# A decode-attention kernel: two loads merged, and matmuls added in TensorE's gaps at the end

## The chip, the cores and the metric

The kernel runs on one core of one Trainium2 chip. The metric is the device time of one execution in microseconds (us), taken over several executions; the span of a profile is about 2 us shorter, because it counts from the first to the last instruction. All runs quoted count as fast runs: the slower state that some programs show plays no part. Below, a "slow run" only means one that took about 1 us or more longer than the fastest of the same kernel. The variants of a group and the kernel before were timed alternately on one chip; the two groups of experiments ran on two different chips, so variants of different groups are compared by way of the kernel before, whose medians there differ by 0.01 us.

## The reference

One decoded token goes through two branches whose outputs are mixed by a scalar gate. Cut to what matters:

```python
q = (x @ wq)                       # 1 x 1024 times 1024 x 4096: 32 heads of 128
scores = q . k_cache / sqrt(128)   # 4 kv heads x 65536 keys x 128
o = softmax(scores) . v_cache      # 4 kv heads x 65536 values x 128
a = o @ wo                         # 4096 x 1024
z = gelu(x @ w_in)                 # 1024 x 3584
z1, z2 = halves of z;  z2 = layernorm(z2)
b = (z1 * (w_sp * z2 + b_sp)) @ w_out
out = g * a + (1 - g) * b          # g = sigmoid(sum(x * gate_w))
```

All inputs are bfloat16. The K and V caches are 134 MB of the 162 MB that have to be read, and every byte is used once: this is a job for the DMA engines.

## The kernel before

All large loads go through one helper. It issues a DMA from SyncE into a slice of one big SBUF buffer of five slots of 4 MB; `at` is the slot. A load can be issued when the readers of the slot's old contents are done.

```python
WO_SPLIT = ((16,), (8, 4, 2, 1, 1))

def load(src, shape, at):
    ...
    v = kv[:, int(at * CT * P):int(at * CT * P) + n]
    ...
    ins = nc.sync.dma_start(out=v, in_=src)
    ...

win_t = [load(win_view[:, i * KH:(i + 1) * KH, :], (KH, F), 3 + i) for i in range(2)]
wq_t = [load(wq_view[:, i * KH:(i + 1) * KH, :], (KH, HD), 1 - i) for i in range(2)]
```

The end of the kernel, which the argument is about: the last V tiles, the last head's normalisation (`head_out`: VectorE steps with two small matmuls between them), and then the output projection, in pieces of `wo` that shrink towards the end so that little work follows the last byte. A "row" of `wo` is here one 1024-column row on each of the 128 partitions, 256 KB. Each row costs four matmuls of 32 output partitions x 256 columns, which run side by side in the four column groups of the array: in the profile before, the four of the last row start within 0.01 us of one another, and each takes 0.37 to 0.40 us.

```python
def project(w, n, vec, c0, first=False, last=False):
    for c in range(n):
        for t in range(NB):                                    # NB = 4
            nc.tensor.matmul(
                out_ps[t * B:(t + 1) * B, :],
                lhsT=vec[:, c0 + c:c0 + c + 1].to_broadcast([P, B]),
                rhs=w[:, c, t * NO:(t + 1) * NO],
                start=(first and c == 0), stop=(last and c == n - 1), ...)

for j, n, at in ((0, 2, 1), (2, 1, 3), (3, 1, 4)):             # the last head's V: 2 + 1 + 1 tiles
    for i, vt in enumerate(load_kv(A_v_cache, G - 1, j, at, n)):
        v_tile(G - 1, j + i, vt)
head_out(G - 1)                                                # makes oa, the vector for wo
...
for at, split in enumerate(WO_SPLIT):
    for n in split:
        t = load(wo_view[:, c0:c0 + n, :], (n, D), at + c0 % (OC // 2) * D / (CT * P))
        project(t, n, oa, c0, last=(c0 + n == OC))
        c0 += n
```

## Time and profile before

| | kernel before |
|---|---|
| median of the first 6 runs | 383.28 us (383.12 to 383.5) |
| span of the profiled run | 381.4 us |
| load queue | 162.01 MB, 98.7% of the 16 DMA engines' span |
| TensorE busy, mean granted clock | 61%, 0.82 |

These are lines of the profile page of the kernel before. In the first two, one character is a fortieth of the span, in tenths; the third gives the load queue's packets, MB and share of the DMA engines' time; the last is the chain of waits by engine.

```profile
...
PEclk9966659998759895989588959895799679969766
DMA  9999999999999999999999999999999999999995
...
q1 hardware_dynamic: 4324, 162.01, 98.7%
...
DMA 59%; PE 20%; DVE 16%; issue 2%; ACT 1%; SPq 1%; DVEq 0%; ACTq 0%
...
```

The DMA engines are busy from start to end, so time can only go where the stream of bytes is not yet or no longer flowing, or where it is slowed. TensorE's granted clock (1.0 is 9 here, 0.5 is 5) rises and falls the whole time.

First, the last steps of the chain of waits (start, duration, what), then the `wo` matmuls on the timeline (start, duration, engine, line, operation, count, and in brackets the idle time before and what ended it), then the windows view: for each stretch its length, the busy time of the engines, the granted clock (PEclk), the DMA share and GB/s.

```profile
...
347.00 31.88 DMA kv<-in_A_wo_dram
...
378.92 0.43 PE out_ps L478 x3
...
379.37 0.37 ACT out_sb L521
...
```

```profile
...
370.37 4.62 PE L478 MATMUL out_ps<-kv,oa 128*32 128x256 bf16 x96 [1.39 <-DVE oa L469]
376.33 0.62 PE L478 MATMUL out_ps<-kv,oa 128*32 128x256 bf16 x16 [1.34 <-DMA kv<-in_A_wo_dram]
377.60 1.08 PE L478 MATMUL out_ps<-kv,oa 128*32 128x256 bf16 x12 [0.64 <-DMA kv<-in_A_wo_dram]
378.92 0.41 PE L478 MATMUL out_ps<-kv,oa 128*32 128x256 bf16 x4 [0.24 <-DMA kv<-in_A_wo_dram]
```

```profile
...
core 0: us, PE busy (x) PEld busy (x) DVE busy (x) ACT busy (x) POOL busy (x), PEclk, DMA share, GB/s
...
371.20:373.60 2.40, 2.40 (x53) 1.85 (x45) 0.00 (x0) 0.00 (x0) 0.00 (x0) 0.50 0.99 413
373.60:376.90 3.30, 1.96 (x56) 1.45 (x49) 0.00 (x0) 0.00 (x0) 0.00 (x0) 0.93 0.94 368
376.90:379.10 2.20, 1.25 (x20) 0.50 (x15) 0.00 (x0) 0.00 (x0) 0.00 (x0) 0.63 0.33 122
...
```

The chain says that from 347.00 to 378.88 the kernel waits for `wo` to arrive. When the last row is there, 0.43 us of matmul and 0.37 us of cast follow, then the output DMA. The timeline says that 96 matmuls, for the first 24 rows, are done by 375, because 16 of the rows were there early (in the DMA packet records their last packet ends at 368.38) and their 64 matmuls could run from 370.37 on. After that TensorE waits for each piece, if only for 0.07 us before the row that starts at 378.28: it is never behind. The windows view says that it does much of that at a granted clock of 0.50.

### The profile page before, as it was taken

How to read it: one execution, taken by the hardware profiler on the slowest of the kernel's cores; microseconds unless marked ns; L12 is line 12 of the kernel's file. 1: busy time of each engine (PE TensorE's matmuls, PEld its weight loads, DVE VectorE, ACT ScalarE, POOL GpSimd, SP SyncE). 2: the span in 40 equal slices, each digit the busy share in tenths (PEclk: the TensorE clock that was granted, in tenths of full speed). 3: DMA queues.
4: the chain of work that ended last, by engine and by line, in shares of the span. 5: the costliest groups of instructions: out<-in, count | busy, mean ns of one | idle time of the engine just before them, and what ended most of it. 6: DMA issues, size and time to landing. Idle time of an engine off the chain costs nothing.

```text
span 381.4 us, 2581 instructions
## 1 busy us (share of the span) xinstructions
PE 232.4 (61%) x1372; PEld 56.8 (15%) x796; DVE 218.4 (57%) x211; ACT 39.6 (10%) x55; POOL 4.4 (1%) x10
## 2 busy tenths in 40 slices
PE   0433467678157944796397629872967196849355
PEld 0110011112011210121011101120111011212123
DVE  4241487996687506966977059669780488550040
ACT  1010001111601100114010001050001010500000
POOL 4000000000000000000000000000000000000000
PEclk9966659998759895989588959895799679969766
DMA  9999999999999999999999999999999999999995
GB/s 376 439 426 416 433 436 440 436 461 429 400 426 440 440 435 426 440 440 440 440 428 440 440 440 433 428 427 406 433 440 428 426 433 427 440 411 436 440 405 230
DMA packets 4375, 162.17 MB, mean 425 GB/s; under 512 B 520, under 2 KB 524, under 8 KB 908
## 3 DMA queue, kind: packets, MB, share of 16 engines
q1 hardware_dynamic: 4324, 162.01, 98.7%
q8 instruction: 8, 0.13, 0.1%
q14 instruction: 3, 0.02, 0.0%
q10 hardware_dynamic: 40, 0.01, 0.0%
HBM read 162.01 MB, written 0.00 MB: 425 GB/s over the span
## 4 chain that ended last, share of the span: by engine, by line
DMA 59%; PE 20%; DVE 16%; issue 2%; ACT 1%; SPq 1%; DVEq 0%; ACTq 0%
DMA kv<-in_A_k_cache_dram 37%; PE s_ps L391 15%; DVE kv L384 9%; DMA kv<-in_A_wo_dram 8%; DMA kv<-in_A_wq_dram 7%; DMA kv<-in_A_v_cache_dram 7%; PE o_ps L437 3%; DVE pt L427 2%; DVE mx L386 1%; DVE o_sb L451 1%; PE q_ps L277 1%; ACT sc L424 1%; DVE rowt L447 1%; ACT sc L402 1%; SPq L167 1%
## 5 line engine op out<-in xcount | busy, mean ns | idle before, releaser
L391 PE MATMUL s_ps<-kv,wt 128*128 128x512 bf16 x512 | 142.1, 437 | 81.8 <-DVE kv L384 81.7
L384 DVE STREAM_TRANSPOSE kv<-kv 128x2048 int32<-128x2048 int32 x64 | 142.7, 2280 | 55.5 <-DMA kv<-in_A_k_cache_dram 55.5
L437 PE MATMUL o_ps<-kv,pt 128*64 128x512 bf16 x512 | 61.6, 399 | 7.7 <-DMA kv<-in_A_v_cache_dram 7.7
L391 PEld LDWEIGHTS <-wt 128*128 128x128 bf16 x256 | 27.5, 108 | 197.6 <-issue 140.2
L402 ACT CAST sc<-s_ps 128x1024 bf16<-128x1024 f32 x16 | 16.2, 1013 | 253.5 <-PE s_ps L391 253.5
L437 PEld LDWEIGHTS <-pt 128*64 128x64 bf16 x256 | 16.0, 115 | 50.7 <-issue 48.1
L427 DVE STREAM_TRANSPOSE pt<-sc 128x1024 bf16<-128x1024 bf16 x16 | 18.6, 1217 | 6.8 <-ACT sc L424 6.8
L386 DVE TENSOR_REDUCE mx<-sc 128x1 f32<-128x1024 bf16 x12 | 14.5, 1207 | 10.1 <-ACT sc L402 10.1
L424 ACT ACTIVATE sc<-sc,nb 128x1024 bf16<-128x1024 bf16 x16 | 18.2, 1137 | 12.2 <-DVE nb L420 12.2
L447 DVE TENSOR_TENSOR rowt<-o_ps,own 128x1024 f32<-128x1024 f32 x4 | 4.8, 1194 | 24.9 <-PE o_ps L437 24.9
L457 PE MATMUL om_ps<-o_sb,hsel 128*32 128x128 f32 x8 | 2.5, 421 | 19.7 <-DVE o_sb L451 19.7
L406 DVE TENSOR_REDUCE mx<-sc 128x1 f32<-128x1024 bf16 x4 | 4.9, 1220 | 14.2 <-ACT sc L402 14.2
L277 PE MATMUL q_ps<-kv,xT 128*32 128x512 bf16 x64 | 7.2, 627 | 7.4 <-DMA kv<-in_A_wq_dram 7.4
L478 PE MATMUL out_ps<-kv,oa 128*32 128x256 bf16 x128 | 6.7, 366 | 3.7 <-DMA kv<-in_A_wo_dram 2.2
L277 PE MATMUL z_ps<-kv,xT 128*32 128x448 bf16 x64 | 6.2, 570 | 3.8 <-DMA kv<-in_B_w_in_dram 3.8
L344 DVE TENSOR_TENSOR rowt<-q_ps,own_b 128x512 f32<-128x512 f32 x2 | 1.3, 686 | 12.5 <-PE q_ps L277 12.5
L451 DVE TENSOR_REDUCE o_sb<-rowt 128x128 f32<-128x1024 f32 x4 | 7.5, 1872 | 0.1
L292 DVE TENSOR_TENSOR rowt<-z_ps,own_b 128x448 f32<-128x448 f32 x2 | 1.2, 620 | 8.5 <-PE z_ps L277 8.5
L233 PE MATMUL xb_ps<-xg,spread 8*128 8x256 bf16 x1 | 0.4, 367 | 9.1 <-DMA xg<-in_gate_w_dram 9.1
L277 PEld LDWEIGHTS <-xT 128*32 128x32 bf16 x64 | 3.0, 139 | 19.4 <-issue 19.3
L478 PEld LDWEIGHTS <-oa 128*32 128x32 bf16 x128 | 4.4, 124 | 6.1 <-issue 3.3
L521 ACT CAST out_sb<-out_ps 128x256 bf16<-128x256 f32 x1 | 0.4, 372 | 45.4 <-PE out_ps L478 45.4
(88 smaller groups left out, 54.8 us busy)
## 6 DMA issues: line engine op xcount, KB each, us to landing
kv<-in_A_k_cache_dram SPq DMA_DIRECT2D x4, 4096.0 KB, 26.8
kv<-in_A_wq_dram SPq DMA_DIRECT2D x2, 4096.0 KB, 32.8
kv<-in_A_v_cache_dram SPq DMA_DIRECT2D x2, 4096.0 KB
kv<-in_B_w_in_dram SPq DMA_DIRECT2D x2, 3584.0 KB, 15.0
kv<-in_A_wo_dram SPq DMA_DIRECT2D x1, 4096.0 KB
kv<-in_B_w_out_dram SPq DMA_DIRECT2D x1, 3584.0 KB
kv<-in_A_wo_dram SPq DMA_DIRECT2D x1, 2048.0 KB, 28.6
kv<-in_A_wo_dram SPq DMA_DIRECT2D x1, 1024.0 KB, 30.7
```

What stands on the lines that cost most here:

```text
L277: ins = nc.tensor.matmul(ps[t * B:(t + 1) * B, k * HN:k * HN + n], lhsT=xT[:, i * KH + c:i * KH + c + 1].to_broadcast([P, B]), rhs=w[:, c, ...
L384: nc.vector.transpose(out=kb[:, v * n:(v + 1) * n], in_=kb[:, v * n:(v + 1) * n])
L386: nc.vector.reduce_max(**late.pop())
L391: ins = nc.tensor.matmul(s_ps[:, k * HN:(k + 1) * HN], lhsT=wt[g % 2][:, v, b].rearrange("p a v h -> p (a v h)"), rhs=kx[:, b // 2, b % 2, ...
L402: nc.scalar.copy(out=sct[g, j][:], in_=s_ps[:])
L406: nc.vector.reduce_max(**late.pop())
L424: nc.scalar.activation(out=sct[g, j][:], in_=sct[g, j][:], func=ACT.Exp, scale=SCALE, bias=nb[:, 0:1], accum_out=lss[g][:, j:j + 1])
L427: nc.vector.transpose(out=ptt[g, j][:].rearrange("p c x -> p (c x)"), in_=sct[g, j][:])
L437: ins = nc.tensor.matmul(o_ps[g][hs, e, :], lhsT=ptt[g, j][:, 2 * u:2 * u + 2, :].rearrange("p c x -> p (c x)"), rhs=vx[:, 2 * u + e], sta ...
L447: nc.vector.tensor_tensor(out=om8, in0=o_ps[g][:].rearrange("p e (v d) -> p (e v) d", d=DH), in1=own_8[:].unsqueeze(2).to_broadcast([P, 2 ...
L451: nc.vector.tensor_reduce(out=o_sb[:], in_=om8.rearrange("p x d -> p d x"), axis=AX.X, op=ALU.add)
L478: nc.tensor.matmul(out_ps[t * B:(t + 1) * B, :], lhsT=vec[:, c0 + c:c0 + c + 1].to_broadcast([P, B]), rhs=w[:, c, t * NO:(t + 1) * NO], st ...
```

## The change

The intent: fewer and larger loads (`w_in` in one, the first 24 rows of `wo` in one), and since TensorE then has gaps, matmuls that are thrown away ("fillers" below) keep it active so that its clock stays full for the 96 matmuls that now follow a single landing. The fillers multiply a weight buffer of which 15 of 16 elements are zero; nobody reads the result. There are 4 after the last V tile, 8 after the last head, and 2, 1 and 1 between the last rows.

```diff
--- before.py
+++ after.py
@@ -22,7 +22,8 @@
 CC = CT // VC
 ZN = 448
 HN = 512
-WO_SPLIT = ((16,), (8, 4, 2, 1, 1))
+WO_SPLIT = (24, 4, 2, 1, 1)
+WO_BUSY = (0, 2, 1, 1, 0)
 
 
 @with_exitstack
@@ -62,7 +63,7 @@
     SCALE = float(DH) ** -0.5
     assert NB * VC * REP == P and G * B == P and B == REP * QD and DH == P and D % P == 0
     assert S % (P * CT) == 0 and F == 2 * NB * ZN and ZN == B * FC and HD == NHB * NB * HN
-    assert NHB * NB == 2 * G and CC * B == 2 * HN and sum(map(sum, WO_SPLIT)) == OC
+    assert NHB * NB == 2 * G and CC * B == 2 * HN and sum(WO_SPLIT) == OC
 
     const = ctx.enter_context(tc.tile_pool(name="const", bufs=1))
     wk = ctx.enter_context(tc.tile_pool(name="wk", bufs=2))
@@ -186,7 +187,8 @@
 
     KH = KC // 2
     win_view = B_w_in.rearrange("(p c) n -> p c n", c=KC)
-    win_t = [load(win_view[:, i * KH:(i + 1) * KH, :], (KH, F), 3 + i) for i in range(2)]
+    win = load(win_view, (KC, F), 3)
+    win_t = [win[:, i * KH:(i + 1) * KH, :] for i in range(2)]
     wq_view = A_wq.rearrange("(p c) n -> p c n", c=KC)
     wq_t = [load(wq_view[:, i * KH:(i + 1) * KH, :], (KH, HD), 1 - i) for i in range(2)]
 
@@ -469,6 +471,15 @@
         nc.vector.tensor_scalar(out=oa[gs, :], in0=osum[gs, :], scalar1=rl[gs, 1:2],
                                 scalar2=gate[gs, :], op0=ALU.mult, op1=ALU.mult)
 
+    def keep_busy(n):
+        ps = pss.tile([P, 2 * HN], FP32, name="busy_ps", tag="s")
+        w = wt[G % 2][:].rearrange("p v b t u h -> p (v b t u h)")
+        for i in range(n):
+            ins = nc.tensor.matmul(ps[:, :HN], lhsT=w[:, :P], rhs=w[:, :HN], start=True,
+                                   stop=True, skip_group_check=True)
+            if i > 0:
+                same_weights(ins)
+
     NO = D // NB
     out_ps = psl.tile([P, NO], FP32, name="out_ps")
 
@@ -506,16 +517,18 @@
     for j, n, at in ((0, 2, 1), (2, 1, 3), (3, 1, 4)):
         for i, vt in enumerate(load_kv(A_v_cache, G - 1, j, at, n)):
             v_tile(G - 1, j + i, vt)
+    keep_busy(4)
     head_out(G - 1)
+    keep_busy(8)
 
 
     wo_view = A_wo.rearrange("(p c) n -> p c n", c=OC)
     c0 = 0
-    for at, split in enumerate(WO_SPLIT):
-        for n in split:
-            t = load(wo_view[:, c0:c0 + n, :], (n, D), at + c0 % (OC // 2) * D / (CT * P))
-            project(t, n, oa, c0, last=(c0 + n == OC))
-            c0 += n
+    for n, busy in zip(WO_SPLIT, WO_BUSY):
+        t = load(wo_view[:, c0:c0 + n, :], (n, D), c0 * D / (CT * P))
+        project(t, n, oa, c0, last=(c0 + n == OC))
+        keep_busy(busy)
+        c0 += n
     out_sb = const.tile([P, NO], BF16, name="out_sb")
     out_rows = out.rearrange("o t (q n) -> (o t q) n", n=NO)
     nc.scalar.copy(out=out_sb[:], in_=out_ps[:])
```

## The prediction

> **What bounds the kernel now.** The DMA stream. The page shows the DMA engines at 9 tenths or more in 39 of 40 slices, the load queue 98.7% busy, 162.0 MB at 425 GB/s over 381.4 us; its chain of waits is 59% DMA. The Trainium skill ("DMA: Bandwidth & Descriptors", "Where 436 GB/s comes from") gives a ceiling of 435 GB/s; the trace agrees (steady slices 426 to 440). Estimate from it: 162.0 MB / 435 GB/s = 372.4 us, so only about 9 us could go at all: 1 us before the first packet, slow first packets, short pauses of single DMA engines, 2 us of unequal finish of the engines, 2.5 us after the last row of wo (timeline: last matmuls 378.92, cast 379.37, output DMA 379.77, end 381.4). PE is 61% busy; at the tail the windows view shows a granted clock of 0.50 to 0.74.
>
> **Removed.** Two loads of 30. In the DMA packet records a 64 KB packet takes 2421 ns, a 32 KB one 1216, so a packet boundary costs about 11 ns; each merge removes eight packets per engine: 16 x 11 = 0.18 us, plus two completion packets of 9 ns. Estimate: 0.2 us off the DMA stream, all critical.
>
> **Moved, off the path.** The first w_in half's matmuls (3.2 us from 12.66) must now wait for all of w_in (about 19.7). The z chain ends 2 to 3 us later, but q's second half lands only at 39.1, and the K load freed by q's first half (issued 33.0) has 16 us of queue ahead of it. The 24-row wo load must wait for the V tile in the next buffer: issued at 345.2 instead of 333.1, with the queue filled until 358.7. No starvation in either.
>
> **Added.** 16 matmuls of 512 columns (0.22 us each at full clock, 0.43 at half). The Trainium skill ("TensorE: Matmul & The Clock Gate", Part 1) describes a free-running window of 3413 ns; the trace agrees (granted stretches are multiples of 3.41 us), and adds: from half clock, windows over 83% busy led to full, under 75% to half; from full clock, under 42% to half. Rows 16 to 23 of wo land at 373.8. Before, 64 of the first 96 matmuls were done by then; now all 96 start there: 24 groups x 0.107 = 2.6 us at full clock, 5.1 at half. The later rows land at 376.3, 377.6, 378.9. At full clock PE catches up, and the last group is 0.1 to 0.2 us shorter. But the 8 fillers end by 370.7 (full) or 372.4 (half), leaving 1.4 to 3 us idle before 373.8, so in some window phases the clock falls just when the 96 start; then fillers between the last rows delay the end by 0.3 to 1.5 us.
>
> **Sum.** -0.2 (DMA), -0.15 (tail at full clock), +0.3 or so averaged over phases, with more spread than before. I expect 383.0 us, 8 in 10 between 382.2 and 384.0: within 2% almost surely.
>
> **What would show it.** Right: load queue still about 98.7% busy; two loads and 256 packets fewer, last landing 0.1 to 0.4 us earlier; first q matmuls 1 to 3 us later but K landings unchanged. The granted clock in 374 to 379 decides: if full, the last project matmuls follow the last landing by under 0.5 us; if half, PE runs without a gap from 373.8 to the end, and the chain names project, not the wo DMA.
>
> **What would make it wrong.** Larger packets changing the DMA rate or the engines' unequal finish by over 1 us; instruction fetches shifting; a K load issued so late that the queue runs empty.

## The result

| | median us | lowest to highest | runs |
|---|---|---|---|
| before | 383.28 | 383.12 to 383.5 | 6 |
| changed | 384.59 | 383.04 to 385.24 | 6 |

The ratio is 1.0028 (95% interval 1.001 to 1.0046). Ratios here are the mean time of one kernel's fast runs over that of the other's of the same rounds, so they are not quite the ratios of the medians quoted. The change made the kernel slower by 0.3% in the ratio, clear of the noise; the median, 384.59, lies above the predicted range of 382.2 to 384.0. The six runs were 383.04, 385.24, 384.61, 384.66, 384.57 and 384.15: one slightly faster than any run before, five slower by 0.9 to 2.0 us.

The profiled run was the fast one, 383.04 us. Its page:

```profile
...
PEclk9997569998659885989598958996889588979789
...
q1 hardware_dynamic: 4036, 162.01, 98.7%
...
```

The load queue is as busy as before, with 288 packets fewer (256 of data and 32 that signal the completion of a load on one engine). The chain of waits, the timeline (the lines with `busy_ps` are fillers) and the windows of this fast run:

```profile
...
346.59 30.78 DMA kv<-in_A_wo_dram
...
378.73 0.32 PE out_ps L489 x4
...
```

```profile
...
369.21 1.90 PE L478 MATMUL busy_ps<-wt 128*128 128x512 bf16 x8
373.64 3.24 PE L489 MATMUL out_ps<-kv,oa 128*32 128x256 bf16 x112 [2.53 <-DMA kv<-in_A_wo_dram]
...
377.41 0.40 PE L489 MATMUL out_ps<-kv,oa 128*32 128x256 bf16 x8 [0.21 <-DMA kv<-in_A_wo_dram]
...
378.73 0.29 PE L489 MATMUL out_ps<-kv,oa 128*32 128x256 bf16 x4
```

```profile
...
371.20:373.60 2.40, 0.00 (x0) 0.00 (x0) 0.00 (x0) 0.00 (x0) 0.00 (x0) 1.00 0.81 338
373.60:376.90 3.30, 3.26 (x113) 3.05 (x112) 0.00 (x0) 0.00 (x0) 0.00 (x0) 1.00 0.92 363
...
```

This is what the change was meant to do. The granted clock is 1.00; the 112 matmuls of the first 28 rows take 3.24 us. The chain waits for `wo` until 377.37 and then follows matmuls and fillers that keep pace with the landings: the last matmuls start at 378.73. In the DMA packet records the last packet of the last row ends at 378.22 us instead of 378.37. So this run explains a gain of 0.2 us, and not the loss. The loss had to be caught in a profile of a slow run.

At the start, the later work on `w_in` is harmless. The timeline of the first 50 us, before and then changed (line 233/235 is the first small matmul, 277/279 the first half of q, 384/386 the first K tile):

```profile
...
9.13 0.37 PE L233 MATMUL xb_ps<-xg,spread 8*128 8x256 bf16 x1 [9.13 <-DMA xg<-in_gate_w_dram]
...
29.39 3.55 PE L277 MATMUL q_ps<-kv,xT 128*32 128x512 bf16 x32 [1.26 <-DMA kv<-in_A_wq_dram]
...
48.83 2.31 DVE L384 STREAM_TRANSPOSE kv<-kv 128x2048 int32<-128x2048 int32 x1 [1.59 <-DMA kv<-in_A_k_cache_dram]
```

```profile
...
13.14 0.36 PE L235 MATMUL xb_ps<-xg,spread 8*128 8x256 bf16 x1 [13.14 <-DMA xg<-in_gate_w_dram]
...
30.23 3.38 PE L279 MATMUL q_ps<-kv,xT 128*32 128x512 bf16 x32
...
48.69 2.31 DVE L386 STREAM_TRANSPOSE kv<-kv 128x2048 int32<-128x2048 int32 x1 [1.53 <-DMA kv<-in_A_k_cache_dram]
```

The first half of q starts 0.84 us later, the first K tile 0.14 us earlier.

### The profile page after: what moved, and what is told of

The parts are those of the page before. It is cut to its first block, busy times and chain, and to the rows that moved or that the text cites. A ratio compares the mean times of both kernels' runs of the same rounds, so it can differ in the third digit from the quotient of the medians.

```text
span 381.1 us, 2597 instructions
## 1 busy us (share of the span) xinstructions
PE 230.6 (60%) x1386; PEld 55.8 (15%) x801; DVE 218.4 (57%) x211; ACT 39.6 (10%) x55; POOL 4.4 (1%) x10
## 3 DMA queue, kind: packets, MB, share of 16 engines
q1 hardware_dynamic: 4036, 162.01, 98.7%
## 4 chain that ended last, share of the span: by engine, by line
DMA 57%; PE 22%; DVE 17%; issue 2%; ACT 1%; ACTq 0%; SPq 0%; DVEq 0%
DMA kv<-in_A_k_cache_dram 37%; PE s_ps L393 15%; DVE kv L386 9%; DMA kv<-in_A_wo_dram 8%; DMA kv<-in_A_v_cache_dram 7%; DMA wb<-in_B_b_sp_dram 5%; PE o_ps L439 3%; DVE pt L429 2%; PE z_ps L279 1%; DVE mx L388 1%; DVE o_sb L453 1%; PE q_ps L279 1%; ACT sc L426 1%; DVE rowt L449 1%; ACT sc L404 1%
## 5 line engine op out<-in xcount | busy, mean ns | idle before, releaser
L393 PE MATMUL s_ps<-kv,wt 128*128 128x512 bf16 x512 | 139.7, 432 | 84.4 <-DVE kv L386 84.3
L439 PE MATMUL o_ps<-kv,pt 128*64 128x512 bf16 x512 | 62.9, 405 | 6.8 <-DMA kv<-in_A_v_cache_dram 6.8
L489 PE MATMUL out_ps<-kv,oa 128*32 128x256 bf16 x128 | 4.2, 273 | 2.8 <-DMA kv<-in_A_wo_dram 2.7
L279 PE MATMUL z_ps<-kv,xT 128*32 128x448 bf16 x64 | 4.9, 484 | 0.0
L489 PEld LDWEIGHTS <-oa 128*32 128x32 bf16 x128 | 3.5, 96 | 5.2 <-issue 3.4
```

The lines of the kernel that those rows point to most:

```text
L279: ins = nc.tensor.matmul(ps[t * B:(t + 1) * B, k * HN:k * HN + n], lhsT=xT[:, i * KH + c:i * KH + c + 1].to_broadcast([P, B]), rhs=w[:, c, ...
L393: ins = nc.tensor.matmul(s_ps[:, k * HN:(k + 1) * HN], lhsT=wt[g % 2][:, v, b].rearrange("p a v h -> p (a v h)"), rhs=kx[:, b // 2, b % 2, ...
L439: ins = nc.tensor.matmul(o_ps[g][hs, e, :], lhsT=ptt[g, j][:, 2 * u:2 * u + 2, :].rearrange("p c x -> p (c x)"), rhs=vx[:, 2 * u + e], sta ...
L489: nc.tensor.matmul(out_ps[t * B:(t + 1) * B, :], lhsT=vec[:, c0 + c:c0 + c + 1].to_broadcast([P, B]), rhs=w[:, c, t * NO:(t + 1) * NO], st ...
```

## The experiments

The fillers are called early (the 4 and the 8 before the landing of the 24 rows) and late (the 2, 1 and 1 between the last rows). The theory (clock): the grant is decided per window of 3.41 us, as the records of the granted clock change only at multiples of that. Where the boundaries of the windows fall in a run is called the phase. The gap between the last early filler and the landing of 24 rows is about as long as a window, so in most phases of the window the clock drops to half as the 96 matmuls start. TensorE then falls behind the landings, and the fillers between the last rows stand in front of data that is already there. Two rivals: the larger packets make the DMA engines slower or finish less evenly; or fillers cost time at any clock.

Each variant ran five times. The kernel before ran beside them nine times for each group of four (the first four and the last four rows of the table): 383.24 us median (383.05 to 383.44) beside the first group, 383.25 (383.14 to 383.42) beside the second. None differs from the kernel before by 2%; a ratio whose interval contains 1 is not told apart from it at all.

| run | early fillers | late fillers | w_in | wo | median us | lowest to highest | ratio (95%) |
|---|---|---|---|---|---|---|---|
| win_only | none | none | 1 load | 16, 8, ... | 383.16 | 383.12 to 383.17 | 0.9998 (0.9986 to 1.0011) |
| wo24_bare | none | none | 1 load | 24, ... | 383.68 | 382.96 to 383.99 | 1.0008 (0.9996 to 1.0021) |
| again (the change) | 4, 8 | 2, 1, 1 | 1 load | 24, ... | 384.39 | 384.36 to 384.63 | 1.0032 (1.0018 to 1.0045) |
| fill18 | 4, 18 | 2, 1, 1 | 1 load | 24, ... | 383.00 | 382.90 to 383.04 | 0.9994 (0.9981 to 1.0006) |
| no_late | 4, 8 | none | 1 load | 24, ... | 383.05 | 382.92 to 384.09 | 1.0004 (0.9992 to 1.0017) |
| late_only | none | 2, 1, 1 | 1 load | 24, ... | 384.82 | 384.08 to 385.40 | 1.0041 (1.0028 to 1.0053) |
| fill18_no_late | 4, 18 | none | 1 load | 24, ... | 383.09 | 382.94 to 383.20 | 0.9994 (0.9981 to 1.0008) |
| wo16_8_fill | 4, 8 | 2, 1, 1 | 1 load | 16, 8, ... | 384.07 | 383.22 to 384.46 | 1.0016 (1.0003 to 1.0028) |

### again: the changed kernel once more

No edit.

> The changed kernel once more, for its spread. Clock theory: which window phase a run gets decides, so times spread from 383.0 to 385.3 us again (median about 384), while the kernel before stays within 0.4 us; if this profile falls in a slow run, the granted clock is 0.5 somewhere in 373.6 to 379 and the 96 project matmuls take over 3.5 us. Rival (larger packets make the DMA engines finish unequally): in a slow profile the last row of wo lands over 1 us later than 378.2 at full clock.

Measured: 384.42, 384.63, 384.37, 384.39, 384.36. Five of five were slow, and the spread was smaller than expected. This time the profile is that of a slow run (384.42). Its chain, timeline and windows:

```profile
...
373.60 4.84 PE out_ps L489 x84
378.44 0.54 PE busy_ps L478 x2
...
379.31 0.32 PE busy_ps L478
...
379.86 0.32 PE busy_ps L478
...
```

```profile
...
368.33 1.90 PE L478 MATMUL busy_ps<-wt 128*128 128x512 bf16 x8
373.60 4.84 PE L489 MATMUL out_ps<-kv,oa 128*32 128x256 bf16 x112 [3.37 <-DMA kv<-in_A_wo_dram]
378.37 0.61 PE L478 MATMUL busy_ps<-wt 128*128 128x512 bf16 x2
378.91 0.40 PE L489 MATMUL out_ps<-kv,oa 128*32 128x256 bf16 x8
...
380.11 0.29 PE L489 MATMUL out_ps<-kv,oa 128*32 128x256 bf16 x4
```

```profile
...
371.20:373.60 2.40, 0.00 (x2) 0.00 (x1) 0.00 (x0) 0.00 (x0) 0.00 (x0) 0.98 0.78 324
373.60:376.90 3.30, 3.30 (x64) 2.85 (x67) 0.00 (x0) 0.00 (x0) 0.00 (x0) 0.50 0.94 370
...
```

Compare it with the fast run of the same code. The 8 early fillers end at 370.23, and nothing is on TensorE until 373.60: 3.37 us. In the granted-clock records, which have a boundary at 373.52 us, the clock falls there to 0.5, and the window 373.6 to 376.9 has 0.50 where the fast run has 1.00. The same 112 matmuls take 4.84 us instead of 3.24. They end at 378.4, when the last packet of `wo` has already landed; the remaining 16 matmuls and the four fillers run one after the other, and the chain goes through all of them: 0.54 + 0.32 + 0.32 = 1.18 us of it is fillers. That packet ended at 378.20, as in the fast run (378.22). The data was not late, so the DMA rival falls for this loss; TensorE was late.

### win_only: only the w_in load merged

```diff
 # kernel before, with
-    win_t = [load(win_view[:, i * KH:(i + 1) * KH, :], (KH, F), 3 + i) for i in range(2)]
+    win = load(win_view, (KC, F), 3)
+    win_t = [win[:, i * KH:(i + 1) * KH, :] for i in range(2)]
```

> Kernel before with w_in as one load, nothing else changed. Clock theory: 0.1 to 0.2 us faster than before (383.1 us), spread under 0.5 us. Rival (larger packets, a later z and x chain): carries part of the loss, 383.6 us or more, or spread over 1 us.

Measured: 383.16, spread 0.05 us. Merging `w_in` carries none of the loss. The gain of 0.1 us agrees with the theory's, but the interval contains 1, so it is not shown.

### wo24_bare: both loads merged, no filler at all

```diff
 # changed kernel, with
-    keep_busy(4)
     head_out(G - 1)
-    keep_busy(8)
 ...
         project(t, n, oa, c0, last=(c0 + n == OC))
-        keep_busy(busy)
```

> The changed kernel with all 16 filler matmuls taken out; w_in is one load and 24 rows of wo are one load. Clock theory: 96 matmuls wait for one landing at a clock that is often half, so 383.0 to 384.3 us with a mean of 383.6, worse than before but better than the change, because no filler stands between the last rows. Rival that the fillers help as intended: slower than the changed kernel. Rival that the DMA is at fault: same as the changed kernel, 384.5.

Measured: 383.68 median, 382.96 to 383.99, so less than the change as it stands: its slowest run is below the fastest run of again (384.36). The fillers as a set made the merged load worse. Against the kernel before the interval contains 1. Its timeline:

```profile
...
367.25 0.41 PE L459 MATMUL om_ps<-o_sb,hsel 128*32 128x128 f32 x2 [3.07 <-DVE o_sb L453]
373.65 6.16 PE L489 MATMUL out_ps<-kv,oa 128*32 128x256 bf16 x128 [6.00 <-DMA kv<-in_A_wo_dram]
```

All 128 matmuls run without a gap for 6.16 us, at a clock of 0.50 until 378.8. They end at 379.84 by the chain, against 379.35 in the profile before, where 64 of them were done early: merging 24 rows leaves TensorE a backlog that half clock doesn't clear in time.

### fill18: a longer bridge

```diff
 # changed kernel, with
-    keep_busy(8)
+    keep_busy(18)
```

> The changed kernel with 18 fillers in place of 8 after the last head, so that TensorE has work until about 373.1 us and no window before the 96 matmuls is nearly empty. Clock theory: clock full from about 365 to the end in every phase, 383.0 us with a spread under 0.5 us. Rivals (DMA, or fillers delaying by themselves): still 384 to 385, or later yet.

Measured: 383.00, spread 0.14 us. The timeline and the windows:

```profile
...
368.49 4.06 PE L478 MATMUL busy_ps<-wt 128*128 128x512 bf16 x18
373.66 3.24 PE L489 MATMUL out_ps<-kv,oa 128*32 128x256 bf16 x112 [1.11 <-DMA kv<-in_A_wo_dram]
...
```

```profile
...
373.60:376.90 3.30, 3.24 (x113) 3.02 (x112) 0.00 (x0) 0.00 (x0) 0.00 (x0) 1.00 0.92 364
...
```

The 18 fillers end at 372.55, 1.11 us before the landing. The granted clock is 1.00, the 112 matmuls take 3.24 us, and with the same late fillers the loss is gone. So late fillers do not cost time whatever the clock: the second rival falls. Ten matmuls more made the kernel 1.4 us faster than the change.

### no_late: the same clock, without the fillers between the rows

```diff
 # changed kernel, with
-WO_BUSY = (0, 2, 1, 1, 0)
+WO_BUSY = (0, 0, 0, 0, 0)
```

> The changed kernel without the four fillers between the last rows of wo; the 4 and 8 fillers before stay. If the loss is those four standing in front of rows that have already landed (a PE that is behind at half clock), runs fall to 383.0 in most phases and at most 384.3 (mean 383.3). If the loss is the 96 matmuls at half clock by themselves, it stays at 384.4. If the rows' fillers keep the clock up for the last group, it gets worse than the change.

Measured: 383.05, 383.02, 382.92, 384.06, 384.09. The profiled run (383.05) had the clock of the slow run of the change:

```profile
...
368.69 1.90 PE L478 MATMUL busy_ps<-wt 128*128 128x512 bf16 x8
373.74 5.38 PE L489 MATMUL out_ps<-kv,oa 128*32 128x256 bf16 x128 [3.15 <-DMA kv<-in_A_wo_dram]
```

```profile
...
373.60:376.90 3.30, 3.17 (x68) 2.89 (x71) 0.00 (x0) 0.00 (x0) 0.00 (x0) 0.58 0.93 365
...
```

The granted clock is half from 374.12 to 377.53, and the 128 matmuls take 5.38 us. They end at 379.14 by the chain, only 0.1 us after those of the fast run of the change (379.05), while the slow run of the change, at nearly the same clock, ended at 380.43. At this clock the four fillers are what costs the time. Two runs still were at 384.1; they have no trace, and the theory's explanation for them (half clock for longer, as in wo24_bare) is argued, not shown.

### late_only: the late fillers without the early ones

```diff
 # changed kernel, with
-    keep_busy(4)
     head_out(G - 1)
-    keep_busy(8)
```

> The changed kernel without the 4 and the 8 fillers, but with the four between the last rows. The clock should be half when the 96 matmuls start in nearly every run, and the four fillers then stand in front of landed rows: 383.5 to 385.3 us, mean 384.4, that is 0.8 above the same kernel with no filler at all (383.68 median). If late fillers are harmless: 383.7.

Measured: 384.82, 384.08 to 385.40; 1.14 us above the same kernel with no filler (which ran in the other group). The timeline of the slowest run:

```profile
...
373.72 5.79 PE L489 MATMUL out_ps<-kv,oa 128*32 128x256 bf16 x112 [5.94 <-DMA kv<-in_A_wo_dram]
379.44 0.60 PE L478 MATMUL busy_ps<-wt 128*128 128x512 bf16 x2
...
```

The backlog reaches to 379.5, later than the last packet (which ended at 378.30), and the late fillers delay what is left. They can't "keep the clock full": the clock had been granted by the backlog's own work, from 378.98 on.

### fill18_no_late

```diff
 # changed kernel, with both edits:
-    keep_busy(8)
+    keep_busy(18)
-WO_BUSY = (0, 2, 1, 1, 0)
+WO_BUSY = (0, 0, 0, 0, 0)
```

> 18 fillers after the last head as in the run before, and none between the last rows. Clock theory: full clock when the 96 start, so PE is never behind; 383.0 us, spread under 0.3, equal to the run with the four late fillers within 0.1 us; if the clock drops for the last group, at most 0.1 us later.

Measured: 383.09, 382.94 to 383.20. With full clock at the start of the 96, late fillers make no difference that these runs resolve. This profile is also the hardest case for the bridge:

```profile
...
367.73 5.75 PE L478 MATMUL busy_ps<-wt 128*128 128x512 bf16 x18
373.68 3.24 PE L489 MATMUL out_ps<-kv,oa 128*32 128x256 bf16 x112 [0.20 <-DMA kv<-in_A_wo_dram]
...
```

The clock fell to half at 368.82, the fillers then took longer (5.75 us), ended at 373.48, and themselves brought the clock back to 1.0 at 372.23, before the 96 matmuls began.

### wo16_8_fill: the old split of wo, with all the fillers

```diff
 # changed kernel, with
-WO_SPLIT = (24, 4, 2, 1, 1)
-WO_BUSY = (0, 2, 1, 1, 0)
+WO_SPLIT = (16, 8, 4, 2, 1, 1)
+WO_BUSY = (0, 0, 2, 1, 1, 0)
```

> The changed kernel, but wo loaded as 16, 8, 4, 2, 1, 1 rows, all fillers kept (4, 8, and 2, 1, 1 after the 4, 2 and 1 rows). Clock theory: 64 of the 96 matmuls run before 373.8 again and themselves keep TensorE busy, so PE is behind by far less: 383.1 to 383.9, mean 383.5. If the merged load as such does not matter and only fillers do: 384.4.

Measured: 384.07, 383.22 to 384.46, with the mean of 383.86 (of 384.07, 383.22, 384.46, 384.22 and 383.35) between the two expectations and three of five runs above 383.9, the highest expected. The timeline:

```profile
...
369.75 1.93 PE L489 MATMUL out_ps<-kv,oa 128*32 128x256 bf16 x64
373.65 1.06 PE L489 MATMUL out_ps<-kv,oa 128*32 128x256 bf16 x32 [1.97 <-DMA kv<-in_A_wo_dram]
376.14 1.05 PE L489 MATMUL out_ps<-kv,oa 128*32 128x256 bf16 x16 [1.44 <-DMA kv<-in_A_wo_dram]
377.12 1.03 PE L478 MATMUL busy_ps<-wt 128*128 128x512 bf16 x2
...
```

Even without a merged `wo` load the fillers hurt. At full clock the 64 matmuls are over in 1.93 us, at 371.68; TensorE then idles for 1.97 us and again for 1.44, and the clock falls at 376.14 just when the last rows come. The two fillers then take 1.03 us by the timeline, and the matmuls of the next rows start at 378.09, where they started at 377.60 in the profile before. So the merge and the fillers each do damage: by medians, the fillers without the wo merge cost 0.91 us (384.07 less 383.16), the merge without fillers 0.52 (383.68 less 383.16), both together 1.23 (384.39 less 383.16). The 0.52 is the least certain of these, since the runs of wo24_bare scatter over 1.0 us.

## Why the prediction was wrong

- **The bound.** Right: the load queue stays at 98.7%, and the small gain in the profiles of the best runs comes about half from the DMA stream and half from the tail (the bullets on both below). The ceiling of 435 GB/s that the prediction took fits the trace as an average to about 1%: of the 40 slices of the page, 13 show 440 and one 461.
- **-0.2 us on the DMA stream.** Right within 0.1: the last packet of `wo` ends 0.08 to 0.18 us earlier in all nine other profiles (378.19 to 378.30, against 378.37), and win_only gains 0.1 us by the medians. The two kernels with only one merge (378.22 and 378.27) lie in the same range, so what each merge gives is not resolved.
- **The w_in chain is off the path.** Right in effect. The delay of the first q matmuls was 0.84 us, a little under the 1 to 3 predicted; the K landing did not move.
- **-0.15 us for a tail at full clock.** Right: fill18 and the fast run end their matmuls 0.3 us earlier than before, 0.15 of it by the landing.
- **"+0.3 or so averaged over phases".** This is the step that failed. The mechanism was named, and the signs given for it were those found: half clock from about 374, project without a gap, a chain that names project, and late fillers that delay the end. The size of the delay (0.3 to 1.5 us in the bad case) was less far off: the median of again is 1.15 above before, and the highest run of the change 2.0. What was mis-sized above all is how often it happens: "in some window phases". Ten of the eleven runs of the change (six and five) were above 384 us, with a mean of 384.40; that is 1.1 over before, where the prediction's terms add up to -0.05 and its 383.0 us stands for -0.3. With the other two terms as they were, the third measured about +1.5, not +0.3. The size had a part in it: counted from the fast run (383.04) the ten slow ones are 1.1 to 2.2 us later, 1.5 in the mean, which is the top of the 0.3 to 1.5 foreseen.
- **What the numbers at hand would have said.** This is an estimate made afterwards, from the trace before. The gap as predicted was 370.7 to 373.8, 3.1 us. A window of 3.41 us that is under about 45% busy loses the clock, so it needs 0.55 x 3.41 = 1.88 us of idle time. Windows with at least so much of the gap can start anywhere in a stretch of 3.1 + 3.41 - 2 x 1.88 = 2.75 us, out of 3.41: 81% of the phases. With the gap of 3.37 us measured in again it is 89%. Both take the phase to be evenly spread. A gap of 3.1 us was listed as a risk and weighted as an exception; it was the rule. The kernel got through in the first profile by the luck of its phase. Its gap was shorter, 2.53 us, because the last V tile ran at half clock until 365.03, ended 0.9 us later than in again (365.66 against 364.76) and so made the fillers late; but by the same estimate 64% of the phases lose the clock in a gap of that length too. Here a boundary at 371.86 cut the gap into 0.75 and 1.78 us, and the window from 371.86 to 375.27 came to 48% busy. The same boundary would have cut the gap of again (370.23 to 373.60) into 1.63 and 1.74 us, neither of them the 1.88 us needed.

Whether the window's phase is evenly spread over runs stays open: the five runs of again lie within 0.27 us of one another, which a random phase would hardly give.

## What to carry to other kernels

The fillers of the merged kernel in one view, medians in us:

| early fillers | no late fillers | late fillers 2, 1, 1 |
|---|---|---|
| none | 383.68 | 384.82 |
| 4, 8 | 383.05 (two of five at 384.1) | 384.39 |
| 4, 18 | 383.09 | 383.00 |

Work that keeps a clock up has to last until the real work starts. Here a gap of 1.1 us was short enough (with 18 early fillers all ten runs lie between 382.90 and 383.20), one of 2.5 us kept the clock by luck, and in gaps of 3.2 and 3.4 us it was lost; a bridge that is too short (4, 8) brought little, with means of 383.43 against 383.54 for none. What made the change worse than no filler at all was the late fillers: work between pieces that wait for data is free only as long as the engine is ahead of the data, so put none where it may be behind. Real work in the gap also served: with 16 rows of `wo` loaded early and no filler, win_only took 383.16 us, with a spread of 0.05. When runs of one version spread more than those of another, profile the slow runs: here the one trace at hand showed the change succeeding.

The best version found, fill18, beat every run of the kernel before (383.04 against 383.05 at the closest), but by 0.06% in the ratio, with an interval that contains 1: it is the same speed, for a kernel that the DMA stream bounds.

## What the Trainium skill lacked or had wrong

- "TensorE: Matmul & The Clock Gate", "HAM oscillation — how this bites in real kernels", says in the abstract that idle gaps must stay under about 3.4 us, and its closing table ("Why this matters for your kernels") under about 3. That is not enough here. In the kernel before, the window from 374.08 to 377.49 had no gap over 1.34 us and was 45% busy, and the clock fell at its end. What told the windows apart was their busy share: over the windows of the ten profiles that begin before 378 us, by TensorE's busy time as the profile models it, all 164 windows after which a half clock became full were 77% busy or more, and all 209 after which it stayed half were 76% or less; 166 of the 167 windows after which a full clock fell were 45% busy or less (one 53%), and all 503 after which it stayed were 41% or more. The window length the page gives, 3413 ns, agrees with every record but the last of each profile, which is cut off at its end.
- "DMA: Bandwidth & Descriptors", "Queues, rings and completion order", says that a DMA engine alternates between queues by whole packets. The runs agree, and give the cost: each small load has a data and then a completion packet on an engine, and in the packet records these four start 1.07 us apart in the kernel before and 2.12 us apart after the change, where one bulk packet takes 1.06 and 2.12 us. With these bulk packets of 57 KB in place of 28 KB, the matmul waiting for two small loads on another queue (2 KB each) started at 13.14 us instead of 9.13 us.
- "DMA: Bandwidth & Descriptors", "Anatomy of one DMA — SWDGE (gpsimd) path", puts most of a fixed cost of about 2 us into what follows the last byte, the write receipt. That section is about loads issued from GpSimd and has no such split for loads issued from SyncE. For these, what follows the last byte was far less than most of 2 us: the last data packet of `wo` in the kernel before ended at 378.37 and the waiting matmuls started at 378.92, 0.55 us later.
